# Starting the output projection's first token block inside the last head pair's attention, on head outputs read back into V's weight buffers, with the last stores split

## The chip, the cores and the metric

The kernel runs on one core of a Trainium2 chip. The metric is the device time of one execution in microseconds (us). A kernel is timed in several rounds, with the kernel before run beside it on the same chip. Medians are quoted with the lowest and highest run. A ratio is the mean time of one kernel's fast runs over the mean of the other's fast runs of the same rounds, so it is not quite the ratio of the medians quoted.

The engines are called by these names: TensorE (PE in the profile, PEld for its weight loads), VectorE (DVE), ScalarE (ACT), GpSimd (POOL), and SyncE's queue (SPq), which issues nearly all DMA transfers, in order.

## The reference, cut to what matters

Two independent parts share the kernel. Part A, a state-space layer, is finished long before the change acts. Part B is attention over 2048 tokens with 32 heads of 128. The part that matters here is its end:

```python
o = jnp.einsum('bhqk,bhke->bhqe', p, v)     # head outputs
o = jnp.einsum('bhte,hed->btd', o, Wo)      # output projection: 32 heads x 128 -> 1024
```

The output projection needs all 32 heads of a token. The kernel goes through the heads in 16 pairs, so no token's projection can be completed before the last pair's attention. It can be begun: the sum over heads can run over the heads that are there.

## The kernel before

Attention works pair by pair. TensorE projects Q and K of the next pair while the current pair's attention runs between those projections. Each pair has 11 units of two token groups each: scores on TensorE, exponential on ScalarE, mask multiplication on GpSimd, values on TensorE, division on VectorE. When a pair is complete, its outputs go to DRAM:

```python
# att_back: at the end of a head pair
if b0 + n == 2 * NG:
    ...
    k.SP.dma_start(on[64:T - 64, :].rearrange("(g p) n -> p g n", p=GX)[:, :, cs], ov[0:GX, 1:NG - 1, :])
    k.SP.dma_start(on[0:64, cs], ov[0:64, 0, :])
    k.SP.dma_start(on[T - 64:T, cs], ov[0:64, NG - 1, :])
    ...
```

`on` has four tensors, one for each quarter of the heads (four pairs). After attention, the projection reads them back transposed, 512 tokens (one of four token blocks) and all four quarters at a time, and multiplies:

```python
def load_o(self, tb):
    t = self.p4.tile([128, H, 512], BF16, name="b_ol", bufs=2)
    ...
    for q in range(4):
        ...  # one transposing DMA for a quarter (three for the last quarter of block 0)
            k.SP.dma_start_transpose(t[...], self.on[q][rows, ...])

def outproj(self, tb, ol):
    ...
    for tt, half in order:             # 4 token tiles x 2 halves of the output columns
        p = k.ps("P")
        for h in range(H):
            PE.matmul(p[:], ol[:, h, tt * 128:(tt + 1) * 128], self.wo[half][:, h, :], start=(h == 0), stop=(h == H - 1))
        k.copy("s" if half else "v", ost[:, hs], p[:])
        ...
```

```python
# driver: attention, and after it everything of the projection
for n, (hp, u) in enumerate(at):
    ...                                # projections of the next pairs are drawn in here
p3.close()
xs.close()                             # frees the input x, Q/K weights and V's weight and staging buffers
with pool("wo1", "left", 1) as wp1, pool("p4", "left") as p4:
    ...
    ol = b.load_o(0)
    tc.keep_in_program_order(k.SP.dma_start(wo1, b.Wo[:, :, 512:D]))
    for tb in range(4):
        nx = b.load_o(tb + 1) if tb < 3 else None
        for _ in b.outproj(tb, ol):
            pass
        ...
```

The framework orders each engine's instructions by when it expects them to be ready. `keep_in_program_order` pins an instruction to its written place. Three accumulators (`ps("P")`) are shared by the Q/K projections and the output projection.

Of the kernel before, what the change touches and what calls it, by code (L numbers as in the profile page):

```python
# [9 lines left out]
BF16 = mybir.dt.bfloat16  # L10
# [13 lines left out]
T = 2048; D = 1024; KC = 8; TT = 16  # L24
PC = 8; TB = 512; NB = 4
H = 32; E = 128; SEG = 32; M = 8; NSEG = 64; L = M + SEG
# [4 lines left out]
NG = 22; GX = 96; GW = 99; NU = NG // 2  # L31
# [3 lines left out]
NMX = 7  # L35
NM = NTL + NMX
NR = 80
EV = E + 1
MW = 4 * GW + 29

# [2 lines left out]
XP = 2128  # L43
# [265 lines left out]
class PartB:  # L309
    def __init__(self, k, x, mem0, Wq, Wk, Wv, Wo, out):  # L310
# [3 lines left out]
        self.Wo = Wo.rearrange("h e d -> e h d")  # L314
        self.vx = [k.drp.tile([NSLOT, 4 * EV], BF16, name=f"b_vx{i}") for i in range(HB)]
        self.vt = [k.drp.tile([NTL, 4 * EV], BF16, name=f"b_vt{i}") for i in range(HB)]
        self.on = [k.drp.tile([T, 1024], BF16, name=f"b_on{i}") for i in range(4)]
        self.tn = [k.drp.tile([NR, 1024], BF16, name=f"b_tn{i}") for i in range(4)]
        c = k.cst
        self.m0T = c.tile([128, KC, M], BF16, name="b_m0T")  # L320
        self.omT = c.tile([128, H, NR], BF16, name="b_omT")
        self.gm = c.tile([NM, D], BF16, name="b_gm")
# [7 lines left out]
    def init(self, tmp):  # L330
# [11 lines left out]
        k.V.memset(self.accR[:], 0.0)  # L342
        z = tmp.tile([32, 4 * EV], BF16, name="b_zero", bufs=1)
        k.V.memset(z[:], 0.0)
# [3 lines left out]
        for q in range(4):  # L348
            k.G.dma_start(self.tn[q][NM:NR, 0:4 * EV], z[0:NR - NM, :])
            k.G.dma_start(self.tn[q][NM:NR, 1024 - 4 * EV:1024], z[0:NR - NM, :])  # L350

# [37 lines left out]
    def v_x(self, hb, w):  # L389
        k = self.k  # L390
        vx = self.vx[hb]
        for q in range(4):
            st = self.wl.tile([128, 4, 4, EV], BF16, name="b_vst", bufs=2)
            k.G.memset(st[:, :, :, E:EV], 1.0)
# [157 lines left out]
    def att_back(self, blocks):  # L552

        k = self.k; PE, V = k.PE, k.V
        hp, b0, n = blocks[0][0], blocks[0][1], len(blocks)
        vt = self.vtile[hp]
        if b0 == 0:
            self.ob = self.p3a.tile([GW, 2 * NG, E], BF16, name="b_ob", bufs=2)
        o = k.ps(("O", "O", "R")[self.nback % 3], (128, 3, EV))
        self.nback += 1  # L560
        for i, (_, b, m, j) in enumerate(blocks):
            PE.matmul(o[:, i, :], m[:, j * GW:j * GW + 128], vt[:, b // 2, (b % 2) * EV:(b % 2 + 1) * EV], start=True, stop=True)
        r = self.accR[0:GW, hp * 2 * NG + b0:hp * 2 * NG + b0 + n]
        V.reciprocal(r, o[0:GW, 0:n, E])
        V.tensor_tensor(self.ob[:, b0:b0 + n, :], o[0:GW, 0:n, 0:E], r.unsqueeze(2).to_broadcast([GW, n, E]), ALU.mult)  # L565
        if b0 + n == 2 * NG:
            del self.vtile[hp]
            q, cs = hp // 4, slice((hp % 4) * 256, (hp % 4) * 256 + 256)
            on, tn = self.on[q], self.tn[q]
            ov = self.ob[:].rearrange("p (g h) e -> p g (h e)", h=2)  # L570
            k.SP.dma_start(on[64:T - 64, :].rearrange("(g p) n -> p g n", p=GX)[:, :, cs], ov[0:GX, 1:NG - 1, :])
            k.SP.dma_start(on[0:64, cs], ov[0:64, 0, :])
            k.SP.dma_start(on[T - 64:T, cs], ov[0:64, NG - 1, :])
            k.SP.dma_start(tn[0:NTL, :].rearrange("(g j) n -> j g n", j=3)[:, :, cs], ov[GX:GW, :, :])
            k.SP.dma_start(tn[NTL:NM, cs], ov[64:64 + NMX, 0, :])
# [23 lines left out]
        yield HP, 0  # L599


    def load_o(self, tb):
        k = self.k
        t = self.p4.tile([128, H, 512], BF16, name="b_ol", bufs=2)
        rows = slice(tb * 512, (tb + 1) * 512)
        for q in range(4):
            for h0, h1 in ((0, 8),) if q < 3 or tb else ((0, 4), (4, 6), (6, 8)):
                k.SP.dma_start_transpose(t[:, 8 * q + h0:8 * q + h1, :], self.on[q][rows, h0 * E:h1 * E])
        return t

    def outproj(self, tb, ol):
        k = self.k; PE = k.PE
        order = [(tt, half) for tt in range(4) for half in range(2)]
        if tb == 0:
            order.sort(key=lambda o: o[1])
        osts = {}
        for tt, half in order:
            t = 4 * tb + tt
            if half == 0:
                osts[tt] = self.p4.tile([128, D], BF16, name="b_ost", bufs=4)  # L620
            ost = osts[tt]
            hs = slice(half * 512, (half + 1) * 512)
            p = k.ps("P")
            for h in range(H):
                PE.matmul(p[:], ol[:, h, tt * 128:(tt + 1) * 128], self.wo[half][:, h, :], start=(h == 0), stop=(h == H - 1))  # L625
            k.copy("s" if half else "v", ost[:, hs], p[:])
            yield
            if half == 1:
                k.SP.dma_start(self.out[0, t * 128:(t + 1) * 128, D:2 * D], ost[:])


    def check(self):
# [142 lines left out]
def kernel_main(tc, A_x, A_Lre, A_Lim, A_Bre, A_Bim, A_Cre, A_Cim, A_logdt, A_Dskip, B_x, B_mem0, B_Wq, B_Wk, B_Wv, B_Wo, out,  # L775
                force=False, dbg=None):
    with ExitStack() as ctx:
        k = K(tc, ctx)
# [4 lines left out]
        b = PartB(k, B_x, B_mem0, B_Wq, B_Wk, B_Wv, B_Wo, out)  # L783

        def pool(name, side, bufs=2):
            return tc.tile_pool(name=name, bufs=bufs, side=side, reuse_waits="tile")
        t32 = ctx.enter_context(pool("t32", "left", 1))
        a.CT = t32.tile([128, 2, PC, D], BF16, name="t32")
        xs = ExitStack()
        xep = xs.enter_context(pool("xe", "left", 1))  # L790
        b.xe = xep.tile([128, KC, XP], BF16, name="b_xe")


        b.wl = xs.enter_context(pool("wl", "left", 1))
        with pool("p1", "right") as p1:
            a.tab = a.tmp = a.wp = a.btp = p1
            wv = b.load_wv(0)
# [9 lines left out]
            for pc in range(PC):  # L807
                v = b.v_x(pc, wv)
# [42 lines left out]
        with pool("p2", "right") as p2:  # L851
            g = b.guess(p2)
# [18 lines left out]
        p3 = ExitStack()  # L871
        b.p3a = p3.enter_context(pool("p3a", "right"))
        b.att_init()
        with pool("p3b", "right") as p3b:
            wo0 = t32.tile([128, H, 512], BF16, name="t32")
            b.qk_init(p3b)
            pr, at = b.proj(), b.attention()
            LEAD = 10
            for _ in range(LEAD):
                next(pr)  # L880
            done = LEAD
            for n, (hp, u) in enumerate(at):
                if n == 12:
                    k.SP.dma_start(wo0[:], b.Wo[:, :, 0:512])
                if u == 4 and hp % 2 == 0 and 2 < hp + 2 < HP:
                    b.v_mem(hp // 2 + 1)
                want = min(18 * HP, LEAD + (n + 1) * 18 // 11)
                while done < want:
                    next(pr)
                    done += 1  # L890
        p3.close()
        xs.close()


        with pool("wo1", "left", 1) as wp1, pool("p4", "left") as p4:
            b.p4 = p4
            wo1 = wp1.tile([128, KC * XP], BF16, name="wo1")
            wo1 = wo1[:, 0:H * 512].rearrange("p (h n) -> p h n", h=H)
            b.wo = (wo0, wo1)
            ol = b.load_o(0)  # L900
            tc.keep_in_program_order(k.SP.dma_start(wo1, b.Wo[:, :, 512:D]))
            for tb in range(4):
                nx = b.load_o(tb + 1) if tb < 3 else None
                for _ in b.outproj(tb, ol):
                    pass
                if tb == 1:
                    for _ in b.check():
                        pass
                ol = nx
# [8 lines left out]
@with_exitstack  # L918
def kernel(
    ctx: ExitStack,  # L920
    tc: tile.TileContext,
    A_x: bass.AP,
    A_Lambda_re: bass.AP,
    A_Lambda_im: bass.AP,
    A_B_re: bass.AP,
    A_B_im: bass.AP,
    A_C_re: bass.AP,
    A_C_im: bass.AP,
    A_log_dt: bass.AP,
    A_Dskip: bass.AP,  # L930
    B_x: bass.AP,
    B_mem0: bass.AP,
    B_Wq: bass.AP,
    B_Wk: bass.AP,
    B_Wv: bass.AP,
    B_Wo: bass.AP,
    B_seg_len: bass.AP,
    out: bass.AP,
):
    assert int(B_seg_len) == SEG  # L940
    kernel_main(tc, A_x, A_Lambda_re, A_Lambda_im, A_B_re, A_B_im, A_C_re, A_C_im, A_log_dt, A_Dskip,
                B_x, B_mem0, B_Wq, B_Wk, B_Wv, B_Wo, out)
# [35 lines left out]
```

## Time and profile before

| | before |
|---|---|
| median (lowest to highest) | 1309.84 us (1308.6 to 1311.27), 3 runs |
| TensorE busy | 1249.8 us, 96% of the profiled span of 1307.5 us |
| last burst of Q/K projection starts | 1037.27 us |
| second token block of the output projection starts | 1118.69 us |
| stretch between the two | 81.42 us |

The stretch from the start of the last 16-matmul projection burst to the first matmul of the second token block holds all that the change moves on TensorE.

The page's 40 slices, each 32.7 us long, show the hole. Each digit is the busy share of a slice in tenths; PEclk is the granted TensorE clock in tenths of full speed.

```profile
PE   6999899999988999999999999999999959999997
...
PEclk9999999999989999999999999999999979999999
```

In the 33rd slice TensorE is half busy, and the clock is down to seven tenths. The TensorE timeline of this stretch tells why. Its columns are the start, the duration, the engine and line, what was written from what, the shape and the count; in brackets stands the idle time before and what ended it. Groups whose members stand close together are merged.

```profile
1037.27 3.40 PE L517 MATMUL psP<-b_xe,b_wk 128*128 128x480 bf16 x16
...
1045.86 1.23 PE L562 MATMUL psO<-b_v,b_m 99*128 99x129 bf16 x6 [0.30 <-POOL b_m L548]
1046.88 0.42 PE L562 MATMUL psR<-b_v,b_m 99*128 99x129 bf16 x2
1059.78 3.19 PE L625 MATMUL psP<-t,b_ol 128*128 128x512 bf16 x7 [12.47 <-DMA b_ol<-b_on]
1063.57 3.63 PE L625 MATMUL psP<-t,b_ol 128*128 128x512 bf16 x16 [0.60 <-DMA b_ol<-b_on]
```

After the last projection burst only the last pair's attention is left, and it runs at GpSimd's pace (six masks of 0.87 us in a row, 5.02 us). Then TensorE waits 12.47 us for the first quarter, and more briefly for the parts that follow (0.60, 0.32, 0.22 and 0.27 us; the last three are not shown). The queue's own timeline shows what it was doing meanwhile:

```profile
1048.24 0.32 SPq L571 DMA_DIRECT2D b_on<-b_ob  x1
1048.78 2.00 SPq L573 DMA_DIRECT2D b_on<-b_ob  x1
1050.83 1.47 SPq L574 DMA_DIRECT2D b_tn<-b_ob  x1
1052.39 8.90 SPq L608 DMA_TRANSPOSE b_ol<-b_on  x2
```

The first read is issued only after the last pair's stores, although three of the four quarters had been in DRAM long before. The same stretch as a table (busy time and number of instructions of each engine, granted clock, busy share of the DMA engines, GB/s):

```profile
core 0: us, PE busy (x) PEld busy (x) DVE busy (x) ACT busy (x) POOL busy (x), PEclk, DMA share, GB/s
1037.27:1040.50 3.23, 3.23 (x19) 1.56 (x17) 1.80 (x4) 0.59 (x2) 0.88 (x1) 1.00 0.00 0
1040.50:1047.30 6.80, 5.00 (x57) 3.28 (x55) 5.66 (x20) 3.33 (x12) 5.02 (x6) 0.91 0.02 4
1047.30:1059.78 12.48, 0.01 (x2) 0.13 (x2) 3.06 (x10) 0.00 (x0) 0.00 (x0) 0.50 0.90 188
1059.78:1071.00 11.22, 9.82 (x36) 3.46 (x36) 0.00 (x0) 0.00 (x0) 0.00 (x0) 0.85 1.12 250
1071.00:1118.69 47.69, 47.35 (x216) 21.40 (x222) 2.77 (x4) 1.79 (x3) 0.00 (x0) 1.00 0.79 199
```

While the attention remainder runs, the DMA engines do nothing (4 GB/s). In the hole they are 90% busy and TensorE does nothing. The two should overlap.

### The profile page before, as it was taken

What the parts mean: (1) busy time and instruction counts of PE and PEld (TensorE: products, weight loads), DVE (VectorE), ACT (ScalarE), POOL (GpSimd) and SP (SyncE); (2) the same over time, 40 slices, a digit from 0 to 9 for tenths busy, and PEclk for the clock granted to TensorE, in tenths of its full rate; (3) what the DMA queues carried; (4) which work ended last, traced back from release to release, by engine and by line L of the source; (5) the groups of instructions that cost most, each with busy time, mean ns of one, the idle gap of its engine ahead of it and who ended that gap; (6) DMA issues with size and microseconds to landing.
All of it is one profiled execution on the core that took longest, in us unless ns stands there. A gap on an engine that the chain in (4) does not pass through costs nothing. (4 is left out here: it accounts for less than half of the span.)

```text
span 1307.5 us, 19151 instructions
## 1 busy us (share of the span) xinstructions
PE 1249.8 (96%) x7630; PEld 649.9 (50%) x7698; DVE 715.3 (55%) x1611; ACT 250.1 (19%) x609; POOL 223.4 (17%) x340
## 2 busy tenths in 40 slices
PE   6999899999988999999999999999999959999997
PEld 2444344444444545555555655555555524444443
DVE  6999999988821124666666666666666610001000
ACT  3343343333310000111111111111111200001000
POOL 7000000000032220222222222222222300000000
PEclk9999999999989999999999999999999979999999
DMA  9994433442399819444464546444543198606000
GB/s 235 243 215 121 121 100 96 129 130 84 103 301 286 258 42 237 105 96 119 97 140 101 135 100 141 101 103 101 108 102 69 34 235 204 154 26 135 17 25 18
DMA packets 312645, 168.88 MB, mean 129 GB/s; under 512 B 140616, under 2 KB 300160, under 8 KB 312552
## 3 DMA queue, kind: packets, MB, share of 16 engines
q1 hardware_dynamic: 310824, 163.91, 50.4%
q0 software_dynamic: 1664, 3.68, 0.9%
q8 instruction: 62, 1.02, 0.3%
q14 instruction: 31, 0.25, 0.1%
q10 hardware_dynamic: 64, 0.02, 0.0%
HBM read 81.18 MB, written 52.19 MB: 102 GB/s over the span
## 5 line engine op out<-in xcount | busy, mean ns | idle before, releaser
L399 PE MATMUL psP<-b_wv,b_xe 128*128 128x512 bf16 x1024 | 230.9, 382 | 15.4 <-DMA b_xe<-in_B_x_dram 10.0
L517 PE MATMUL psP<-b_xe,b_wq 128*128 128x480 bf16 x1024 | 223.0, 366 | 0.0
L517 PE MATMUL psP<-b_xe,b_wk 128*128 128x480 bf16 x1024 | 222.9, 366 | 0.0
L548 POOL TENSOR_TENSOR b_m<-b_e,maskB 99x396 bf16<-99x396 bf16 x160 | 139.4, 872 | 336.1 <-ACT b_e L545 336.1
L545 ACT ACTIVATE b_e<-psS 99x396 bf16<-99x396 f32 x176 | 88.2, 501 | 546.9 <-PE psS L542 543.6
L399 PEld LDWEIGHTS <-b_xe 128*128 128x128 bf16 x1024 | 100.4, 98 | 138.7 <-DMA b_xe<-in_B_x_dram 10.5
L625 PEld LDWEIGHTS <-b_ol 128*128 128x128 bf16 x1024 | 99.9, 98 | 136.8 <-DMA b_ol<-b_on 16.7
L67 DVE CAST b_k<-psP 128x480 bf16<-128x480 f32 (+1 forms) x192 | 98.2, 533 | 100.0 <-PE psP L517 95.6
L67 DVE CAST b_q<-psP 128x480 bf16<-128x480 f32 (+1 forms) x192 | 98.2, 533 | 94.4 <-PE psP L517 92.6
L517 PEld LDWEIGHTS <-b_wk 128*128 128x128 bf16 x1024 | 97.8, 98 | 95.8
L517 PEld LDWEIGHTS <-b_wq 128*128 128x128 bf16 x1024 | 96.6, 98 | 87.9
L625 PE MATMUL psP<-t,b_ol 128*128 128x512 bf16 x500 | 114.4, 383 | 14.5 <-DMA b_ol<-b_on 13.9
L67 DVE CAST b_ost<-psP 128x512 bf16<-128x512 f32 x16 | 11.1, 692 | 207.7 <-PE psP L625 207.7
L297 PE MATMUL psO<-t,a_hl 128*128 128x512 bf16 x497 | 114.3, 385 | 8.9 <-DVE a_ot L299 4.2
L625 PE MATMUL psP<-wo,b_ol 128*128 128x512 bf16 x502 | 112.1, 379 | 0.5
L65 ACT ACTIVATE b_vst<-psP 128x512 bf16<-128x512 f32 x128 | 74.3, 590 | 96.6 <-PE psP L399 73.8
L565 DVE TENSOR_TENSOR b_ob<-psO,b_accR 99x384 bf16<-99x384 f32 x160 | 85.9, 554 | 2.4
L297 PEld LDWEIGHTS <-a_hl 128*128 128x128 bf16 x512 | 49.9, 99 | 68.4 <-issue 6.9
L228 PEld LDWEIGHTS <-a_bt 128*128 128x128 bf16 x512 | 50.1, 99 | 65.6 <-issue 6.1
L299 DVE TENSOR_TENSOR a_ot<-psO,a_xd 128x512 bf16<-128x512 f32 x32 | 21.9, 691 | 107.1 <-PE psO L297 80.3
L542 PEld LDWEIGHTS <-b_k 128*128 128x128 bf16 x704 | 49.9, 98 | 33.1 <-issue 0.5
L228 PE MATMUL psS<-a_xT,a_bt 128*128 128x512 bf16 x232 | 58.8, 382 | 5.6 <-DMA a_xT<-in_A_x_dram 4.7
(195 smaller groups left out, 1086.6 us busy)
## 6 DMA issues: line engine op xcount, KB each, us to landing
b_v<-b_vx SPq DMA_DIRECT2D x16, 1064.2 KB
b_wv<-in_B_Wv_dram SPq DMA_DIRECT2D x16, 1024.0 KB
b_on<-b_ob SPq DMA_DIRECT2D x16, 960.0 KB
b_vx<-b_vst SPq DMA_DIRECT2D x24, 516.0 KB
a_hs<-a_h SPq DMA_DIRECT2D x32, 256.0 KB
b_wq<-in_B_Wq_dram SPq DMA_DIRECT2D x16, 512.0 KB
b_wk<-in_B_Wk_dram SPq DMA_DIRECT2D x16, 512.0 KB
b_wog<-in_B_Wo_dram SPq DMA_DIRECT2D x4, 2048.0 KB
```

Of the source, the lines that this page charges most:

```text
L65: self.S.activation(out, in_, ACT.Copy)
L67: self.V.tensor_copy(out, in_)
L228: PE.matmul(u[:], self.bt[:, i, c, :], self.xT[:, c, tb * TB:(tb + 1) * TB], start=(c == 0), stop=(c == KC - 1))
L297: PE.matmul(py[:], hl[pc // 2][:, pc % 2, i, tt * 128:(tt + 1) * 128], self.CT[:, i, pc, hs], start=(pc == 0 and i == 0), stop=(pc == PC - ...
L299: V.tensor_tensor(ot[:, hs], py[:], xd[:, hs], ALU.add)
L399: k.PE.matmul(p[:], self.xe[:, c, t * 128:(t + 1) * 128], w[:, c, :], start=(c == 0), stop=(c == KC - 1))
L517: PE.matmul(p[:, 0:480], w[i][:, c, hh * 128:(hh + 1) * 128], self.xe[:, c, 480 * q:480 * q + 480], start=(c == 0), stop=(c == KC - 1))
L542: PE.matmul(s[:, gg, hh, :], kt[:, hh, g0:g0 + 128], qt[:, hh, g0:g0 + GW], start=True, stop=True)
L545: k.S.activation(e[:], s[0:GW], ACT.Exp, scale=float(E) ** -0.5, accum_out=self.accE[0:GW, i:i + 1])
L548: k.G.tensor_tensor(m[:, 0:4 * GW].rearrange("p (a b q) -> p a b q", a=2, b=2), e[:], mask[0:GW, :, :].unsqueeze(2).to_broadcast([GW, 2, 2 ...
L565: V.tensor_tensor(self.ob[:, b0:b0 + n, :], o[0:GW, 0:n, 0:E], r.unsqueeze(2).to_broadcast([GW, n, E]), ALU.mult)
L625: PE.matmul(p[:], ol[:, h, tt * 128:(tt + 1) * 128], self.wo[half][:, h, :], start=(h == 0), stop=(h == H - 1))
```

## The change

The intent is to have three of the four quarters of token block 0 on chip before attention ends, and to project on them while the last pair is finished. Four things change:

1. Quarters 0 to 2 of block 0 are read into buffers that V's weights and V's staging no longer need. That takes no new memory.
2. Projection matmuls for three token tiles run over the first 24 heads, in groups of four between the last attention units. Only then do they need quarter 3.
3. The last pair's stores are split, so that the first six of 22 groups, which hold the first 512 tokens, are stored early. Quarter 3 of block 0 depends on these alone.
4. Wo's second half is loaded as soon as the Q/K projections are done, into memory that x held.

```diff
+GE = 6
@@ att_back
+        early = hp == HP - 1
+        def rows(g0, g1):
+            r = on[64 + GX * (g0 - 1):64 + GX * (g1 - 1), :].rearrange("(g p) n -> p g n", p=GX)
+            k.SP.dma_start(r[:, :, cs], ov[0:GX, g0:g1, :])
+        if early and b0 + n == 2 * GE:
+            rows(1, GE)
+            k.SP.dma_start(on[0:64, cs], ov[0:64, 0, :])
         if b0 + n == 2 * NG:
-            k.SP.dma_start(on[64:T - 64, :]...[:, :, cs], ov[0:GX, 1:NG - 1, :])
-            k.SP.dma_start(on[0:64, cs], ov[0:64, 0, :])
+            if early:
+                rows(GE, NG - 1)
+            else:
+                rows(1, NG - 1)
+                k.SP.dma_start(on[0:64, cs], ov[0:64, 0, :])
 ... (cut)
+    def load_o_early(self, q):
+        if q < 2:
+            t = [self.wl.tile([128, 8, 512], BF16, name="b_wv", bufs=2)[:]]
+        elif q == 2:
+            t = [self.wl.tile([128, 4, 512], BF16, name="b_vst", bufs=2)[:] for _ in range(2)]
+        else:
+            t = [self.p4a.tile([128, 8, 512], BF16, name="b_ol3", bufs=1)[:]]
+        self.load_o(0, q, t)
+        self.ol0 += [p[:, h, :] for p in t for h in range(p.shape[1])]
 ... (cut)
+    def outproj_first(self):
+        for tt in range(3):
+            ps.append(k.ps("P"))
+            for h in range(0, 24, 4):
+                self.out_mm(ps[tt], self.ol0, tt, 0, h, h + 4)
+                yield
+        for tt in range(3):
+            for h in range(24, H, 4):
+                self.out_mm(ps[tt], self.ol0, tt, 0, h, h + 4)
+                yield
+            self.out_fin(ps[tt], 0, tt, 0, osts)
+        ... (the other five accumulations of block 0, cut)
@@ driver
+            if hp == 13 and u in (3, 6, 9):
+                b.load_o_early(u // 3 - 1)
 ... (cut)
+            if done == 18 * HP:                  # Q/K projections are all issued
+                if first is None:
+                    xs.close()
+                    b.p4a = ctx.enter_context(pool("p4a", "left", 1))
+                    wo1 = b.p4a.tile([128, H, 512], BF16, name="wo1")
+                    b.wo = (wo0, wo1)
+                    b.load_o_early(3)
+                    for h in range(0, H, 16):
+                        k.SP.dma_start(wo1[:, h:h + 16, :], b.Wo[:, h:h + 16, 512:D])
+                    first = b.outproj_first()
+                next(first)
```

Line numbers shift by one or more between the two kernels: L517, L542, L562 and L625 of before are L518, L543, L563 and L642 after; the stores at L571 to L575 are at L574 to L587, and the transposing read at L608 is at L620.

More of the change, by code (lines that the diff above doesn't have):

```diff
@@ L565, in att_back @@
         V.tensor_tensor(self.ob[:, b0:b0 + n, :], o[0:GW, 0:n, 0:E], r.unsqueeze(2).to_broadcast([GW, n, E]), ALU.mult)
+        q, cs = hp // 4, slice((hp % 4) * 256, (hp % 4) * 256 + 256)
+        on, tn = self.on[q], self.tn[q]
+        ov = self.ob[:].rearrange("p (g h) e -> p g (h e)", h=2)
+        early = hp == HP - 1
[5 more added lines that the diff above has]
+            k.SP.dma_start(on[0:64, cs], ov[0:64, 0, :])
         if b0 + n == 2 * NG:
             del self.vtile[hp]
-            q, cs = hp // 4, slice((hp % 4) * 256, (hp % 4) * 256 + 256)
-            on, tn = self.on[q], self.tn[q]
-            ov = self.ob[:].rearrange("p (g h) e -> p g (h e)", h=2)
-            k.SP.dma_start(on[64:T - 64, :].rearrange("(g p) n -> p g n", p=GX)[:, :, cs], ov[0:GX, 1:NG - 1, :])
-            k.SP.dma_start(on[0:64, cs], ov[0:64, 0, :])
+            if early:
[3 more added lines that the diff above has]
+                k.SP.dma_start(on[0:64, cs], ov[0:64, 0, :])
             k.SP.dma_start(on[T - 64:T, cs], ov[0:64, NG - 1, :])
@@ L599, in attention, with load_o @@
         yield HP, 0
-    def load_o(self, tb):
-        k = self.k
-        t = self.p4.tile([128, H, 512], BF16, name="b_ol", bufs=2)
-        rows = slice(tb * 512, (tb + 1) * 512)
-        for q in range(4):
-            for h0, h1 in ((0, 8),) if q < 3 or tb else ((0, 4), (4, 6), (6, 8)):
-                k.SP.dma_start_transpose(t[:, 8 * q + h0:8 * q + h1, :], self.on[q][rows, h0 * E:h1 * E])
-        return t
+    def load_o(self, tb, q, t):
+        rows = slice(tb * 512, (tb + 1) * 512)
+        h0 = 0
+        for p in t if isinstance(t, list) else [t]:
+            n = p.shape[1]
+            self.k.SP.dma_start_transpose(p, self.on[q][rows, h0 * E:(h0 + n) * E])
+            h0 += n
@@ new lines, in load_o_all @@
+    def load_o_all(self, tb):
+        t = self.p4.tile([128, H, 512], BF16, name="b_ol", bufs=2)
+        for q in range(4):
+            self.load_o(tb, q, t[:, 8 * q:8 * q + 8, :])
+        return [t[:, h, :] for h in range(H)]
+    def load_o_early(self, q):
[7 more added lines that the diff above has]
+        self.ol0 += [p[:, h, :] for p in t for h in range(p.shape[1])]
@@ new lines, in out_mm, with out_fin @@
+    def out_mm(self, p, ol, tt, half, h0, h1):
+        for h in range(h0, h1):
+            self.k.PE.matmul(p[:], ol[h][:, tt * 128:(tt + 1) * 128], self.wo[half][:, h, :], start=(h == 0), stop=(h == H - 1))
+    def out_fin(self, p, tb, tt, half, osts):
+        k = self.k
+        if half == 0:
+            osts[tt] = self.p4a.tile([128, D], BF16, name="b_ost", bufs=4)
+        k.copy("s" if half else "v", osts[tt][:, half * 512:(half + 1) * 512], p[:])
+        if half == 1:
+            t = 4 * tb + tt
+            k.SP.dma_start(self.out[0, t * 128:(t + 1) * 128, D:2 * D], osts[tt][:])
@@ new lines, in outproj_first @@
+    def outproj_first(self):
+        k = self.k
+        osts, ps = {}, []
+        for tt in range(3):
[8 more added lines that the diff above has]
+            self.out_fin(ps[tt], 0, tt, 0, osts)
+        for tt, half in [(3, 0)] + [(tt, 1) for tt in range(4)]:
+            p = k.ps("P")
+            for h in range(0, H, 4):
+                self.out_mm(p, self.ol0, tt, half, h, h + 4)
+                yield
+            self.out_fin(p, 0, tt, half, osts)
@@ L611, in outproj @@
     def outproj(self, tb, ol):
-        k = self.k; PE = k.PE
-        order = [(tt, half) for tt in range(4) for half in range(2)]
-        if tb == 0:
-            order.sort(key=lambda o: o[1])
+        k = self.k
         osts = {}
-        for tt, half in order:
-            t = 4 * tb + tt
-            if half == 0:
-                osts[tt] = self.p4.tile([128, D], BF16, name="b_ost", bufs=4)
-            ost = osts[tt]
-            hs = slice(half * 512, (half + 1) * 512)
-            p = k.ps("P")
-            for h in range(H):
-                PE.matmul(p[:], ol[:, h, tt * 128:(tt + 1) * 128], self.wo[half][:, h, :], start=(h == 0), stop=(h == H - 1))
-            k.copy("s" if half else "v", ost[:, hs], p[:])
-            yield
-            if half == 1:
-                k.SP.dma_start(self.out[0, t * 128:(t + 1) * 128, D:2 * D], ost[:])
+        for tt in range(4):
+            for half in range(2):
+                p = k.ps("P")
+                self.out_mm(p, ol, tt, half, 0, H)
+                self.out_fin(p, tb, tt, half, osts)
+                yield
@@ L788, in kernel_main @@
         a.CT = t32.tile([128, 2, PC, D], BF16, name="t32")
+        b.wl = ctx.enter_context(pool("wl", "left", 1))
         xs = ExitStack()
@@ L791, in kernel_main @@
         b.xe = xep.tile([128, KC, XP], BF16, name="b_xe")
-        b.wl = xs.enter_context(pool("wl", "left", 1))
         with pool("p1", "right") as p1:
@@ L873, in kernel_main @@
         b.att_init()
-        with pool("p3b", "right") as p3b:
-            wo0 = t32.tile([128, H, 512], BF16, name="t32")
-            b.qk_init(p3b)
-            pr, at = b.proj(), b.attention()
-            LEAD = 10
-            for _ in range(LEAD):
-                next(pr)
-            done = LEAD
-            for n, (hp, u) in enumerate(at):
-                if n == 12:
-                    k.SP.dma_start(wo0[:], b.Wo[:, :, 0:512])
-                if u == 4 and hp % 2 == 0 and 2 < hp + 2 < HP:
-                    b.v_mem(hp // 2 + 1)
-                want = min(18 * HP, LEAD + (n + 1) * 18 // 11)
-                while done < want:
-                    next(pr)
-                    done += 1
+        p3b = p3.enter_context(pool("p3b", "right"))
@@ new lines, in kernel_main @@
+        wo0 = t32.tile([128, H, 512], BF16, name="t32")
+        b.qk_init(p3b)
+        pr, at = b.proj(), b.attention()
+        LEAD = 10
+        for _ in range(LEAD):
+            next(pr)
+        done = LEAD
+        first, b.ol0 = None, []
+        for n, (hp, u) in enumerate(at):
+            if n == 12:
+                k.SP.dma_start(wo0[:], b.Wo[:, :, 0:512])
+            if u == 4 and hp % 2 == 0 and 2 < hp + 2 < HP:
+                b.v_mem(hp // 2 + 1)
+            if hp == 13 and u in (3, 6, 9):
+                b.load_o_early(u // 3 - 1)
+            want = min(18 * HP, LEAD + (n + 1) * 18 // 11)
+            while done < want:
+                next(pr)
+                done += 1
+            if done == 18 * HP:
[9 more added lines that the diff above has]
+                next(first)
@@ L891, in kernel_main @@
         p3.close()
-        xs.close()
-        with pool("wo1", "left", 1) as wp1, pool("p4", "left") as p4:
+        with pool("p4", "left") as p4:
             b.p4 = p4
-            wo1 = wp1.tile([128, KC * XP], BF16, name="wo1")
-            wo1 = wo1[:, 0:H * 512].rearrange("p (h n) -> p h n", h=H)
-            b.wo = (wo0, wo1)
-            ol = b.load_o(0)
-            tc.keep_in_program_order(k.SP.dma_start(wo1, b.Wo[:, :, 512:D]))
-            for tb in range(4):
-                nx = b.load_o(tb + 1) if tb < 3 else None
+            ol = b.load_o_all(1)
+            for _ in first:
+                pass
+            for tb in range(1, 4):
+                nx = b.load_o_all(tb + 1) if tb < 3 else None
```

## The prediction

> **What bounds the kernel now.** TensorE: 96% busy (table of busy time), with one hole late in the 40-slice table, which the timeline resolves. The last projection burst ends at about 1040.6 us. What is left of the last head pair's attention (six score groups, 32 value blocks) runs to 1047.3, paced by the GpSimd mask multiplies (0.87 us each). Then the queue issues the stores of the head outputs (1048.24 to 1052), then the transposing reads; the first output-projection matmul starts at 1059.78 after a 12.47 us wait for b_ol. Waits of 0.60, 0.32, 0.22 and 0.27 us follow as quarters land (3.9 us per 1 MB), and seven matmuls take 3.19 us instead of 1.5, since the granted clock was 0.50 until about 1063. The Trainium skill, "TensorE: Matmul & The Clock Gate", Part 1, describes this half rate after a few idle microseconds; the trace agrees.
>
> From 1040.5 to 1118.7, where the second token block starts, 78.2 us pass. Work in it: 256 matmuls at a pitch of 0.2158 us (32 take 6.905) = 55.2 us, and attention leftovers of 6 x 0.18 + 32 x 0.06 = 3.0 us. So 20 us are removable: the ceiling.
>
> **What the change does.** TensorE's work is the same. Quarters 0 to 2 of token block 0 are read back one or more head pairs earlier, into buffers whose V work is over; the instruction order places these transposes around the starts of pairs 11 and 13 (893, 961), before idle queue stretches (976 to 994). Eight groups of four projection matmuls stand between the last attention units, 40 more follow on the same quarters, and only then is quarter 3 needed. The last stores are split so that quarter 3 depends on the first six of 22 groups.
>
> Per unit TensorE then needs 0.86 + 0.36 = 1.22 us, more than GpSimd's 0.87, so the mask chain hides; I allow 0.5 us for the last unit.
>
> Quarter 3 (estimate from the trace): its store is issued at about 1038.6, half of the second weight matrix (2 MB; 4 MB took 12 us at 340 GB/s) goes ahead at about 1041, so the transpose lands near 1054. TensorE needs it at 1040.5 + 72 x 0.2158 + 3.5 = 1059.5. The second weight half lands near 1060, needed near 1074; the next block's reads near 1082, needed at 1099. All hidden.
>
> **Sum.** Block 0 ends at 1040.5 + 55.2 + 3.0 + 0.5 = 1099.2, so 19.4 us earlier; the 188.8 us after it are the same instructions. All of it lies on the critical path. 1309.8 - 19.3 = **1290.5 us**, a gain of 1.5%. Range 1287.5 to 1295.5. Chances: faster by over 2% 0.02, within 2% 0.97, slower 0.01. Even the ceiling is short of 2% (26 us).
>
> **What would show it.** Right: no TensorE wait over 1 us between 1040 and 1100; clock 1.00 throughout; new matmuls starting near 1041 on b_wv; block 0 finished near 1099; the last masks about 1.2 us apart instead of 0.87. Wrong: a TensorE wait on b_ol3 or on the second weight matrix; head pairs 11 to 14 longer than 33.4 us because the early transposes delay V or Q/K loads.
>
> **What would make it wrong.** Quarter 3's store landing late, or its transpose sharing bandwidth with the weight load (up to 5 us lost); TensorE waiting on masks or accumulators in the interleaved stretch (1 to 3 us); early transposes holding up the single issuing queue.

## The result, and the profile after

| | before | after |
|---|---|---|
| median (lowest to highest) | 1309.49 us (1308.6 to 1311.27), 4 runs | 1289.66 us (1288.54 to 1291.9), 4 runs |
| ratio to before | | 0.9855, 95% interval 0.9837 to 0.9873 |
| last projection burst starts | 1037.27 us | 1039.09 us |
| second token block starts | 1118.69 us | 1101.90 us |
| the stretch | 81.42 us | 62.81 us |

The stretch is 18.6 us shorter. The profiled run of after entered it 1.8 us later than that of before. This comes from a wait for V at the start of attention, which both kernels have and whose length varies from run to run (experiment 7). Most of it is not the wait itself (1.97 us after, 1.28 before) but the half clock that followed it in this run of after.

The slices of after, read as above:

```profile
PE   6899899999989999999999999999999999999997
...
PEclk9999999999999999999999999999999999999999
```

The hole and the dip of the clock are gone. TensorE's timeline of after, the groups that answer to those shown of before:

```profile
1039.09 3.40 PE L518 MATMUL psP<-b_xe,b_wk 128*128 128x480 bf16 x16
1042.33 1.03 PE L642 MATMUL psP<-t,b_wv 128*128 128x512 bf16 x4
...
1052.45 0.29 PE L563 MATMUL psO<-b_v,b_m 99*128 99x129 bf16 x2 [0.41 <-POOL b_m L549]
...
1060.46 1.89 PE L642 MATMUL psP<-t,b_vst 128*128 128x512 bf16 x8
1062.19 5.34 PE L642 MATMUL psP<-t,b_ol 128*128 128x512 bf16 x24
```

The projection on the first quarter (now in `b_wv`) follows the last burst with no gap. Quarter 3 (`b_ol` in the last line) is used at 1062.19 with no wait. The only TensorE waits of the stretch are three for a mask, 0.83 us together, the longest the 0.41 us shown. The queue after:

```profile
1040.30 0.32 SPq L574 DMA_DIRECT2D b_on<-b_ob  x1
1042.53 0.40 SPq L953 DMA_DIRECT2D wo<-in_B_Wo_dram  x1
1043.10 10.86 SPq L620 DMA_TRANSPOSE b_ol<-b_on  x1
1054.00 0.58 SPq L953 DMA_DIRECT2D wo<-in_B_Wo_dram  x1
1054.69 1.84 SPq L574 DMA_DIRECT2D b_on<-b_ob  x1
```

The early part of the stores (first line) leaves 14 us before the rest (last line). The read of quarter 3 is issued behind 2 MB of weights. Its issue alone occupies the queue for 10.86 us, so the second 2 MB of weights are issued at 1054.00 only. They are needed at 1077.73 (heads 16 and on of the second half), and TensorE never waits for them. The table of the stretch:

```profile
1039.09:1042.33 3.24, 3.24 (x19) 1.56 (x17) 1.81 (x4) 0.59 (x2) 0.87 (x1) 1.00 0.31 74
1042.33:1052.69 10.36, 9.53 (x85) 5.67 (x84) 6.33 (x18) 3.55 (x12) 5.23 (x6) 1.00 0.96 228
1052.69:1062.19 9.50, 9.50 (x47) 4.30 (x45) 1.59 (x5) 0.00 (x0) 0.00 (x0) 1.00 1.10 315
1062.19:1101.90 39.71, 39.71 (x185) 18.01 (x184) 4.41 (x9) 1.79 (x3) 0.00 (x0) 1.00 1.16 237
```

TensorE is busy 61.98 of 62.81 us, at full clock, while the DMA engines move 228 to 315 GB/s beside it from 1042.33 on. In the row 1042.33 to 1052.69, 28 projection matmuls (28 x 0.2158 = 6.0 us) leave 4.3 us for the attention remainder, which took 6.8 us before.

The early reads did no harm earlier. They are written two pairs ahead of the last one, and the framework issued them earlier still, at 876.11 and 944.32 us. The big stores of successive pairs, which mark the pairs' lengths, stand at 859.52, 894.52, 927.79, 962.79 and 996.05 us after, and at 857.68, 892.68, 925.95, 960.95 and 994.23 us before. The distances are the same to 0.02 us.

### The profile page after: what moved, and what is told of

It reads as the page before. It is cut to its first block, busy times and chain, and to the rows that moved or that the text cites. A ratio compares the mean times of both kernels' runs of the same rounds, so it can differ in the third digit from the quotient of the medians.

```text
span 1290.2 us, 19225 instructions
## 1 busy us (share of the span) xinstructions
PE 1252.3 (97%) x7698; PEld 649.9 (50%) x7698; DVE 716.2 (56%) x1611; ACT 250.7 (19%) x609; POOL 223.7 (17%) x340
## 5 line engine op out<-in xcount | busy, mean ns | idle before, releaser
L518 PE MATMUL psP<-b_xe,b_wk 128*128 128x480 bf16 x1024 | 224.1, 367 | 0.0
L518 PE MATMUL psP<-b_xe,b_wq 128*128 128x480 bf16 x1024 | 223.1, 366 | 0.0
L518 PEld LDWEIGHTS <-b_wk 128*128 128x128 bf16 x1024 | 98.0, 98 | 96.4 <-issue 1.0
L518 PEld LDWEIGHTS <-b_wq 128*128 128x128 bf16 x1024 | 96.7, 98 | 88.0 <-issue 0.2
L642 PEld LDWEIGHTS <-b_ol 128*128 128x128 bf16 x832 | 81.3, 98 | 98.0
L642 PE MATMUL psP<-wo,b_ol 128*128 128x512 bf16 x416 | 92.4, 379 | 0.0
L642 PE MATMUL psP<-t,b_ol 128*128 128x512 bf16 x416 | 92.2, 379 | 0.0
L543 PEld LDWEIGHTS <-b_k 128*128 128x128 bf16 x704 | 50.2, 98 | 34.2 <-issue 0.5
```

The lines of the kernel that those rows point to most:

```text
L518: PE.matmul(p[:, 0:480], w[i][:, c, hh * 128:(hh + 1) * 128], self.xe[:, c, 480 * q:480 * q + 480], start=(c == 0), stop=(c == KC - 1))
L543: PE.matmul(s[:, gg, hh, :], kt[:, hh, g0:g0 + 128], qt[:, hh, g0:g0 + GW], start=True, stop=True)
L642: self.k.PE.matmul(p[:], ol[h][:, tt * 128:(tt + 1) * 128], self.wo[half][:, h, :], start=(h == 0), stop=(h == H - 1))
```

## The experiments

Each result below quotes the median, the ratio to the kernel before of the same rounds, and the stretch from the profile. The yardsticks are 81.42 us (before) and 62.81 us (after).

| run | median us (lowest to highest) | ratio to before (95%) | stretch us |
|---|---|---|---|
| after, first measurement | 1289.66 (1288.54 to 1291.9) | 0.9855 (0.9837 to 0.9873) | 62.81 |
| 1 after, again | 1290.38 (1289.36 to 1293.36) | 0.9849 (0.9828 to 0.987) | 62.81 |
| 2 after attention, pinned | 1295.14 (1294.44 to 1295.98) | 0.9888 (0.9872 to 0.9904) | 66.28 |
| 3 after attention, free | 1290.58 (1289.2 to 1291.23) | 0.9845 (0.9825 to 0.9865) | 62.67 |
| 4 whole last stores | 1297.32 (1295.28 to 1298.95) | 0.99 (0.9883 to 0.9917) | 69.77 |
| 5 heads in order | 1296.18 (1294.68 to 1300.84) | 0.99 (0.9882 to 0.9919) | 70.16 |
| 6 late reads | 1294.97 (1294.15 to 1296.31) | 0.9887 (0.9871 to 0.9903) | 66.42 |
| 7 Wo's first half later | 1288.65 (1287.09 to 1289.18) | 0.9828 (0.9808 to 0.9848) | 62.81 |
| 8 before, kept busy, 46 | 1309.94 (1308.53 to 1314.59) | 1.0001 (0.9979 to 1.0022) | 81.39 |
| 9 before, kept busy, 34 | 1313.29 (1311.13 to 1314.42) | 0.9995 (0.9982 to 1.0009) | 81.70 |
| 10 whole stores, kept busy | 1297.53 (1297.32 to 1297.88) | 0.9882 (0.9867 to 0.9897) | 67.83 |
| 11 two small steps | 1290.14 (1288.6 to 1291.41) | 0.9823 (0.981 to 0.9837) | 62.22 |

Runs 2, 4, 5 and 6 shared a chip (before: 1310.13 us), runs 1, 3, 7 and 8 another (before: 1310.3 us), and runs 9, 10 and 11 a third, on which before took 1313.36 us. So medians of that third chip are compared by ratio.

The theory: the gain is the hole, filled. The reads no longer stand behind the last stores, so TensorE has work from the last burst on, and every part of the change that is taken away brings back the wait that it removed. Rivals: the filling of the mask-bound attention units alone is the gain; reading two pairs ahead is the gain; or the clock, which was at half speed after the hole, is a large part of it.

### 1. The changed kernel again

No edit.

> The changed kernel itself, unaltered, as the yardstick on the same chip for the runs beside it. Expected 0.985 to 0.987 of the kernel before, about 1290 us.

Measured: 1290.38 us, ratio 0.9849, the stretch again 62.81 us. The result repeats on another chip.

### 2. Projection matmuls only after attention, pinned

```diff
-                next(first)
         p3.close()
@@ out_mm
-            self.k.PE.matmul(p[:], ol[h]...)
+            mm = self.k.PE.matmul(p[:], ol[h]...)
+            if ol is self.ol0:
+                self.k.tc.keep_in_program_order(mm)
```

> The changed kernel with its projection matmuls held back until the last attention matmul (reads, split stores and the order of heads unchanged). Theory (the hole closes because the reads of quarters 0 to 2 are done before attention ends; standing between the attention units adds only what TensorE idles there): attention's remainder again takes 6.8 us as before the change, instead of 4.3 us, so 2 to 4 us slower than the changed kernel, about 1292 us, and no TensorE wait on a read. Rival (the filling of the mask-bound last units is the main part of the 19 us): 8 us or more slower, 1298 us or more.

Measured: a stretch of 66.28 us, 3.5 us longer than after, and a median 4.8 us above that of run 1, which was timed on another chip. No wait on a read. The TensorE timeline of this run, and a row of its table (the clock is the third number from the end):

```profile
1041.13 0.34 PE L543 MATMUL psS<-b_q,b_k 128*128 128x99 bf16 x4
...
1047.72 4.82 PE L642 MATMUL psP<-t,b_wv 128*128 128x512 bf16 x16
...
1059.28 3.62 PE L642 MATMUL psP<-t,b_wv 128*128 128x512 bf16 x16
```

```profile
1047.00:1048.00 1.00, 0.96 (x6) 0.65 (x7) 0.73 (x4) 0.00 (x0) 0.25 (x1) 0.50 1.09 371
```

The remainder takes 6.59 us (1041.13 to 1047.72) against 4.3 us, so 2.3 us are lost there. Another 1.2 us come from the first 16 matmuls, which took 4.82 us where a later group of 16 took 3.62. The granted clock was 0.50 from 1047 to 1050, although no gap had been longer than 0.62 us. The theory's wait is right and its sum was short by that clock. The interleaving is worth 3.5 us of the 18.6, so the rival that makes it the main part falls.

### 3. The same, but free to be moved

```diff
-                next(first)
         p3.close()
```

> The changed kernel with its projection matmuls written after attention, but not pinned there: the instruction order of the built program shows that 13 of them are then moved up singly into TensorE's gaps of the last attention units. Theory (what counts is that data and accumulators are ready; any placement that fills the gaps will do): the block from the last projection burst to the second token block within 1 us of the changed kernel's 59.6 us. Rival (the hand-placed groups of four are needed): 2 to 4 us longer, like the pinned run.

Measured: 62.67 us, 1290.58 us, no different from the changed kernel. The framework moved projection matmuls up into the gaps: in the trace 14 stand before the last attention matmuls, one to three at a time (13, singly, in the instruction order that I had read). One such group:

```profile
1045.77 0.81 PE L642 MATMUL psP<-t,b_wv 128*128 128x512 bf16 x3
```

That did as well as the 28 placed by hand, so the hand placement is not needed. What matters, it seems, is that operands and accumulators are ready at that time.

### 4. The last stores whole

```diff
-        early = hp == HP - 1
+        early = False
@@ driver
-                    b.load_o_early(3)
 ... (after the attention loop)
+        b.load_o_early(3)
         p3.close()
```

> The changed kernel with the last pair's stores whole again, and quarter 3 read after them. Theory: the store is issued near 1054.5, and in the kernel before, 11.5 us passed from that issue to the first matmul on a transposed quarter, so quarter 3 lands near 1066 where TensorE needs it at 1062.2: one wait of 3 to 5 us on b_ol3, total 1292 to 1295 us. Rival (the split is idle decoration, the 72 matmuls on the other quarters cover it): no wait, 1290 us. Second rival (quarter 3 needs the split altogether): a wait of 8 us or more.

Measured: 69.77 us, 7.0 us longer, 1297.32 us. The TensorE timeline:

```profile
1066.28 7.52 PE L642 MATMUL psP<-t,b_ol 128*128 128x512 bf16 x24 [4.62 <-DMA b_ol<-b_on]
```

The wait is 4.62 us, inside the 3 to 5 us expected. The 24 matmuls after it took 7.52 us, where the same 24 of after took 5.34. These 2.2 us were not in my sum, and the total lies above the range expected. The split is needed.

### 5. Heads in order, quarter 3 needed after 24 matmuls

```diff
-        for tt in range(3):                       # heads 0 to 23 of three tiles, then their heads 24 to 31
-            ...
-        for tt, half in [(3, 0)] + [(tt, 1) for tt in range(4)]:
+        for tt, half in [(tt, 0) for tt in range(4)] + [(tt, 1) for tt in range(4)]:
```

The matmuls are pinned as in run 2; left free, the framework would move other tiles' matmuls ahead of the wait.

> The changed kernel with the heads of each accumulator in order, so that quarter 3 is needed after 24 matmuls and not after 72 (order pinned). The wait measures when quarter 3 really lands. Theory: it is needed near 1052.5 and lands near 1055.5 (my reading of the traffic in the changed kernel's trace), so one wait of 2 to 4 us on b_ol3, total 1292 to 1295 us. If it lands as late as 1060, the wait is 7 us, and the 5 us to spare of the prediction were not there.

Measured: 70.16 us, 7.35 us longer, 1296.18 us, which lies above the range expected. The TensorE timeline:

```profile
1035.18 3.40 PE L518 MATMUL psP<-b_xe,b_wk 128*128 128x480 bf16 x16
...
1052.67 3.60 PE L642 MATMUL psP<-t,b_ol 128*128 128x512 bf16 x8 [3.72 <-DMA b_ol<-b_on]
1056.06 4.55 PE L642 MATMUL psP<-t,b_wv 128*128 128x512 bf16 x16
```

Quarter 3 is usable 17.49 us after the start of the last burst (1052.67 - 1035.18). Laid over the changed kernel, whose burst starts at 1039.09, that is 1056.6 us, and TensorE there needs it at 1062.19. So 5.6 us were to spare; the prediction had it landing near 1054 and needed at 1059.5, which is 5.5 us. The wait, 3.72 us, lies inside the 2 to 4 us expected. Most of the rest of the loss is the clock again: 3.60 and 4.55 us for groups that take 1.89 and 3.62 at full clock, 2.6 us together. The waits for masks add 0.7 us (1.53 us in all instead of 0.83); here 24 matmuls stand between the attention units, not 28.

### 6. The early reads issued late

```diff
-            if hp == 13 and u in (3, 6, 9):
-                b.load_o_early(u // 3 - 1)
@@ driver, once the Q/K projections are all issued
-                    b.load_o_early(3)
+                    for q in range(4):
+                        b.load_o_early(q)          # each read of block 0 pinned
```

> The changed kernel with the reads of quarters 0 to 2 issued only after the last projection matmul's stores (order pinned), ahead of quarter 3 and the second weight half matrix. Theory: the first 1 MB lands near 1046.5, then 3.9 us per MB, TensorE stands at 1042.3, so waits of 4 us and some 1.5 us, and perhaps 1 us of half clock: 5 to 8 us slower than the changed kernel, 1295 to 1298 us. Rival (reading early is the whole gain): 15 us or more slower, 1305 us or more. Rival (reading early brings nothing, only the order of work does): 1290 us.

Measured: 66.42 us, 3.6 us longer than after; the median is 4.6 us above that of run 1. The waits that I expected did not come (the projection's matmuls are at L644 in this run):

```profile
1046.46 4.40 PE L644 MATMUL psP<-t,b_wv 128*128 128x512 bf16 x12
...
1055.50 1.04 PE L644 MATMUL psP<-t,b_vst 128*128 128x512 bf16 x4 [0.24 <-DMA b_vst<-b_on]
```

The framework put all but the last five matmuls of the attention remainder first. The first quarter was there when TensorE turned to it at 1046.46, and the only wait for a read was 0.24 us. But these first 12 matmuls took 4.40 us, where 12 take 2.75 at full clock (after, from 1052.69). That is 1.7 of the 3.6 us; most of what is left is the remainder, which nothing filled until then. The stretch is close to that of run 2, in which nothing stands between the attention units. So reading ahead of the last pair is worth 3.6 us here, half of it clock. The other 15 us come without it, so the rival that makes it the whole gain falls. What counts most is that the reads are issued before the last pair is finished, and not behind its last stores.

### 7. Wo's first half later

In the traces of before and after, the first value matmuls of attention wait for V (1.28 us before, 1.97 us after, profiled runs). V's stores and loads stand in the queue behind 4 MB of Wo. The lines of after, with the slow matmuls that followed:

```profile
522.09 0.51 PE L563 MATMUL psO<-b_v,b_m 99*128 99x129 bf16 x6 [1.97 <-DMA b_v<-b_vt]
522.44 2.98 PE L518 MATMUL psP<-b_xe,b_wk 128*128 128x480 bf16 x8
```

```diff
-            if n == 12:
-                k.SP.dma_start(wo0[:], b.Wo[:, :, 0:512])
+            if n == 24:
+                tc.keep_in_program_order(k.SP.dma_start(wo0[:], b.Wo[:, :, 0:512]))
```

> The changed kernel with the first half of Wo (4 MB, now loaded just before attention begins) loaded from the second head pair on. In the traces so far the first value matmul of attention waits 1.2 to 2.0 us for V, whose stores and loads stand behind these 4 MB in the queue, and after the longest of these waits eight matmuls took 2.98 us instead of 1.78. Theory: the wait goes, and the kernel is 1.2 to 3.5 us faster than the changed kernel, 1287 to 1289 us. Rival (V's own round trip through DRAM sets the wait): nothing changes.

Measured: 1288.65 us, 1.7 us under run 1 beside it, with ranges that do not overlap (1287.09 to 1289.18 against 1289.36 to 1293.36); the intervals of the ratios do overlap. In the trace the wait for V is gone and the stretch is unchanged. This is the same fault as the hole, in small: a read that is needed soon stands behind one that is not.

### 8 and 9. The kernel before, with TensorE kept busy in the hole

```diff
+        pd = k.ps("R")
+        for _ in range(46):                        # 34 in run 9
+            tc.keep_in_program_order(k.PE.matmul(pd[:], k.ones[:], wo0[:, 0, :], start=True, stop=True))
         p3.close()
```

> The kernel before with 46 matmuls of no use (results never read) put into the hole, pinned between the last attention matmul and the first projection matmul. Theory (part of the 19 us is the half clock after the hole): the first seven projection matmuls run at the full pitch, 1.5 to 3 us faster than before, about 1307.5 us, while the wait for the reads stays where it was. Rival (the slow first matmuls come from reads that trickle in, not from the clock): no change, 1309.5 us.

Measured: no change (ratio 1.0001, 81.39 us). The matmuls of no use were held up by 1.58 us for their accumulator and ran until 1062.6, past the landing of the reads, so the run could not decide. With 34 of them:

> The kernel before with 34 instead of 46 matmuls of no use in its hole; the 46 ran until 1062.6, past the landing of the reads, and so gave back what the clock won. Theory: they end before the reads land, the first matmuls run at the full pitch, and the stretch from the last projection burst to the second token block is 1.3 to 2 us shorter than the 81.4 us of before, about 1308 us. Rival (half clock is not what costs there): 81.4 us again.

Measured: again no change (0.9995, 81.70 us), with a clean trace this time:

```profile
1064.42 1.90 PE L625 MATMUL psP<-t,b_ol 128*128 128x512 bf16 x8 [1.03 <-DMA b_ol<-b_on]
1068.43 3.63 PE L625 MATMUL psP<-t,b_ol 128*128 128x512 bf16 x15 [2.10 <-DMA b_ol<-b_on]
```

The first eight matmuls run at full pitch (1.90 us for eight), so the clock had indeed been what slowed them. But what they win they wait away for the next quarter: 2.10 us where before waited 0.60. In the kernel before, the arrival of the quarters set the pace, and half clock cost nothing. My expectation fails, and so does the rival that gives the clock a share of the 18.6 us.

### 10. Whole stores, with TensorE kept busy in the wait

```diff
 ... run 4, with the matmuls of block 0 pinned, and between heads 0 to 23 and heads 24 to 31:
+        pd = k.ps("R")
+        for _ in range(20):
+            k.tc.keep_in_program_order(k.PE.matmul(pd[:], k.ones[:], self.wo[0][:, 0, :], start=True, stop=True))
```

> The run with whole last stores, with 20 matmuls of no use put into its 4.6 us wait for quarter 3. There the 24 matmuls after the wait took 7.52 us instead of 5.34. Theory (a wait costs its length and then half clock): quarter 3 comes as late as before, but the 24 matmuls take about 5.3 us, and the stretch from the last projection burst to the second token block shrinks from 69.8 to 67.4 to 68.0 us; total about 1295 us. Rival (the slow matmuls come from reads that are still arriving): still 7 us and more.

Measured: 67.83 us (69.77 without), ratio 0.9882 (0.99). The TensorE timeline:

```profile
1061.97 4.48 PE L666 MATMUL psR<-t,ones 128*128 128x512 bf16 x20
1066.99 5.35 PE L642 MATMUL psP<-t,b_ol 128*128 128x512 bf16 x23 [0.54 <-DMA b_ol<-b_on]
```

L666 are the matmuls of no use; one of the 24 records of the last line is missing. Quarter 3 comes as late as in run 4 (28.1 us after the start of the burst, against 27.9), and the matmuls after it are at full pitch. Here nothing later waits for data, so the clock's 2 us are real. The stretch shows it; the intervals of the two ratios overlap, so the times alone do not.

### 11. Two small steps

```diff
 ... run 7, and in attention(), ahead of the last blocks:
+        yield HP, -1
         back(0)
```

The extra step puts one more group of four projection matmuls ahead of the last value blocks.

> The changed kernel with Wo's first half loaded later (as in the run of that name) and with one more group of four projection matmuls ahead of the very last value blocks, where TensorE still waited 0.41 us for the last mask. Expected: the stretch 62.4 instead of 62.8 us, no wait for V, total 1 to 3 us under the changed kernel, about 1288 us, 0.982 to 0.983 of the kernel before; the second step alone is too small for the times to show.

Measured: 62.22 us, no wait for V, mask waits of 0.4 us instead of 0.8, ratio 0.9823. It is the lowest ratio of all runs, but its interval touches that of the first measurement of after, and overlaps that of run 1. The trace shows the two waits gone. That the kernel is faster than after by some 0.3% is likely, not proven, because after was not run on this chip.

## Why the prediction was right

- **The hole and its size.** Predicted: 20 us removable, 19.4 of them removed. Measured: the stretch fell from 81.42 to 62.81 us, 18.6 us; the medians differ by 19.8 us, and the ratio of 0.9855 is 19.0 us of 1309.5. Predicted time 1290.5 us, measured 1289.66 us. That the two are so close is partly luck: the runs of after alone spread over 3.4 us.
- **The matmuls.** Predicted 256 x 0.2158 = 55.2 us. The stretch of 62.81 us less the burst (3.24) and the attention remainder (4.3) leaves 55.3 us. (The 4.3 us were got with the same pitch; the 228 matmuls from 1052.69 to 1101.90 alone, 49.21 us, confirm it.)
- **The attention remainder.** Predicted 3.0 us of work and 0.5 us of waiting. It took 4.3 us, of which 0.83 us are three waits for masks. I had looked at the last unit only; two earlier units waited as well (0.18 and 0.24 us). The other 0.5 us lie just before these waits, where the last matmuls run to their end with nothing behind them (two value matmuls take 0.28 us there, at 0.06 us each in the sum). The masks came on average every 1.44 us (1044.31 to 1051.52 for six), not every 1.2. Seven groups of four stood between the units, not eight; the eighth followed the last one. This is the one mis-sized term, by 0.8 us.
- **Quarter 3 in time.** Predicted 5.5 us to spare, and run 5 measured 5.6 us. The agreement is closer than its two terms: counted from the burst, quarter 3 came and was needed some 0.8 us later than predicted. Runs 4 and 5 show that both measures that buy this time, the split and the order of heads, are needed: 7 us each without them.
- **Everything on the critical path.** What follows the stretch took as long as before, to 0.5 us: from the second block's start to the span's end, 1290.2 - 1101.9 = 188.3 us after and 1307.5 - 1118.7 = 188.8 us before.
- **No harm earlier.** The pairs kept their lengths. The early reads were issued half a pair earlier than I read from the instruction order (876 and 944 us, not near 893 and 961), with no effect.
- **What I had wrong in the mechanism.** I read the seven slow matmuls after the hole (3.19 us instead of 1.5) as a part of the cost. Run 9 showed that they cost before nothing, since the next quarter was late anyway. The sum was not touched, because it came from the whole idle time. And "the trace agrees" with the clock's rule was too quick: the table of before has the clock at 0.91 in the row that ends at 1047.30. It fell while attention was still issuing matmuls, before the idle microseconds.

The parts taken away one at a time cost 3.5 us (interleaving), 7.0 (split), 7.35 (order of heads) and 3.6 (early reads). They don't add up to the gain, and need not: the first and the last are, it seems, much the same loss, and each of the four contains slow matmuls (1.2, 2.2, 2.6 and 1.7 us). In the clock records of the packed traces every stretch at half clock, but for the one at the end of the program, lasts a multiple of 3.41 us (3.41 in runs 2 and 6, 6.83 in runs 4 and 5, 17.07 in before), so one fall can cost a busy TensorE some 1.7 us (an estimate, half of 3.41; run 6 lost as much). About 15 us remain whichever of the first and the last is taken away. By elimination they belong to the reads that no longer wait for the last stores: the waits of before for its reads add up to 13.9 us, and run 2 has none. No run reversed that alone, and none took away the fourth part of the change, the earlier load of Wo's second half.

## What to carry to other kernels

Where a phase begins with a read-back of what the phase before stored, look at the issuing queue: reads of data that was stored long ago may stand behind the last stores for no reason but order. Read the parts that are complete first, begin the sum over them, and split the last store so that what the first step needs is stored first. If the scheduler may move instructions, having operands and accumulators free in time can be enough, as in run 3. A wait can cost its length plus slow matmuls after it (4.62 us and 2.2 us in run 4), but the slow matmuls cost nothing where something later waits for data anyway (run 9): keep the engine busy in one experiment to tell the two apart.

## What the Trainium skill lacked or had wrong

- "TensorE: Matmul & The Clock Gate", Part 1, has the clock fall to half after an idle window of about 3.4 us, and "Why this matters for your kernels" asks for no idle gaps over about 3 us. The runs here show falls without such a gap. In before and in run 2 the clock went to 0.50 between 1046 and 1047 us, in a stretch where TensorE was 74% busy (5.00 of 6.80 us in before) and no gap exceeded 0.62 us. In after's profiled run it went to 0.50 after a gap of 1.97 us at the start of attention: eight matmuls took 2.98 us instead of 1.78. In run 2 a gap of 1.88 us at the same place did nothing. The page calls the window free-running, which allows for such chance, and it also tells of a kernel whose clock oscillates because TensorE idles briefly and often between groups of matmuls, without a figure. As limits on a single gap its figures are too wide.
- The same page tells what a cold start costs; I found nothing on it about when that cost is hidden. Run 9 has it at nothing where later reads set the pace, and run 10 at about 2 us where they don't (stretch 67.83 against 69.77 us).
- "DMA: Bandwidth & Descriptors", "Latency and other measured facts", gives 261 GB/s for transposing DMAs with a non-contiguous middle dimension, and about 350 to 400 for contiguous ones. The trace of before has 250 GB/s in the row 1059.78 to 1071.00, which is nearly all transposes. That is near the first figure; which of the two cases these reads are was not settled.
- I found on no page how long the issue of a transposing DMA can hold the issuing queue: 10.86 us in after, behind 2 MB of weights, which kept the next load from being issued until 1054.00 us, against 3.88 us for a read of the same size in run 6 with no weights ahead of it. That the queue was held until the weights ahead had drained is my reading; no run tests it.
